# First batch's keys and queries prepared side by side in borrowed buffers, mostly transposed by DMA, with weight steps placed behind score tiles

## The chip, the cores and the metric

The kernel runs on one core of a Trainium2 chip. The metric is the time on the device in microseconds (us). The engines are TensorE (PE, with its weight loads shown apart as PEld), VectorE (DVE), ScalarE (ACT), GpSimd (POOL) and SyncE (SP). SP and ACT issue the DMAs: SP the transposes and the stores, ACT the loads.

## The reference

The inputs are `q`, `k`, `v` of 4 batches x 8 heads x 768 rows x 64, 16 `centroids` for each head, and two weights that arrive as 64-bit words.

```python
q_assign = argmax(q_n . c_n)      # q_n, k_n, c_n: normed; per head, 16 clusters
k_assign = argmax(k_n . c_n)
mask     = q_assign[..., :, None] == k_assign[..., None, :]
scores   = where(mask, q @ k.T / 8, -1e9);  attn = softmax(scores)
x = (attn @ v)  ->  3072 tokens x 512          # heads side by side
h = x @ w_in;   g = max(h, 0) + log1p(exp(-|h|));   out = g @ w_out   # 2048 wide
```

So each row of a query sees only the keys of its own cluster, and a softplus feed-forward follows.

## The kernel before, in words

All large products run in fp16 as a high and a low half. The mask is put into the product: a transposed key or query has 128 rows, of which 64 hold the values (T0: low and high half; T1: the high half beside 16 mask columns of -65504 or 0), so that scores come out masked.

Work is cut into 8 passes: batch b, and three of its six row tiles (`QT = 3`). A pass has 8 heads x 3 = 24 score tiles of 128 x 768. For a tile, `scores` does four matmuls (L544), the row maximum on DVE (`negm`, L560) and the exponential on ACT (L568). In pass 0 the probabilities stay in fp32, are transposed on PE (L585) and copied out by ACT and DVE (L591, L593); from pass 1 on they are split into halves on ACT and POOL (`phl`, L607, L609), and two tiles at a time, 24 blocks of 128 x 128, are transposed by a DMA into `pt`. `attend` multiplies by `v` (L647 in pass 0, L651 to L653 afterwards), and `xn` is transposed by DMA into `xT`. `ffn1` (L720 to L722), `softplus` (L739 to L763) and `ffn2` (L784 to L786) of a pass run while later passes attend.

Preparation. `prep_k(n)` takes two heads of a batch: load, high half on ACT (L423), low half on POOL (L425) into a tile `n1`; transpose into `kt[:, 0]`; similarities with the centroids on PE (L394, L395); nearest centroid on DVE (L399 to L403, L440), the mask columns (L444) and a copy into a second tile `n2`; transpose into `kt[:, 1]`. `clusters` counts with a matmul (L456) which clusters have a key (`al`, L461, L464). `prep_q(n, pi)` does the same for four heads and three row tiles (L481, L485, then DVE steps and POOL's product L516). Below, k0, k2, k4, k6 are the four key pairs of batch 0, and q0, q4 its two query groups for pass 0. `turn` transposes 12 blocks, either by DMA or, for `n < NPE` (8: all of batch 0), on PE with two copies out of PSUM (L376, L380, L382). There are two `n1` and two `n2` buffers, two `raw` ones, four `kt`, two `qt`; PSUM has two banks `h` (transposes, similarities, `ffn1`), and one `o` for `ffn2`.

`prep_weights(step)` turns 64-bit words into fp16 halves: ACT, three DVE operations (L305, L309, L315), ACT, POOL (L319), in 32 steps: 16 for `w_in`, 16 for `w_out`. The words are staged in rooms of `wo` that are not yet needed; the last two steps stage in a buffer `wraw` of the ring `phl`.

The order on each engine is set before the run by a planner, `Order`. Each piece of work is a generator that yields operations with an engine and a cost in ns, and waits. The planner always emits the operation that can start first by its own prices; among equals the lower priority number goes first. `wait` and `ring` belong to the planner: they fix when it may emit. The semaphores in the program come from the data alone. Engines then run in the order emitted. Before, a transpose was priced at

```python
self.dma = max(self.dma, start + 900) + opt["dma"]     # 180 ns a block
end = max(self.dma, start + ns) + 1500
```

and a weight step had priority `begin - 12 + step * 0.6`, that is 22 + 0.6 step, where tile t has priority t.

Of the kernel before, what the change touches and what calls it, by code (L numbers as in the profile page):

```python
# [19 lines left out]
DDS = 1024  # L20
LAG = 4
AHEAD = 10
NPE = 8
# [4 lines left out]
class Order:  # L28
# [8 lines left out]
    def __init__(self):  # L37
        self.free = dict.fromkeys(self.LAT, 0.0)
        self.ev, self.blocked, self.active = {}, {}, []
        self.dma = 0.0  # L40
        self.shared = {"DVE": 0.0, "POOL": 0.0}
        self.rings = {}
        self.cur, self.seq = None, 0
# [7 lines left out]
    def get(self, tag, size):  # L51

        k = self.rings.get(tag, 0)
        self.rings[tag] = k + 1
        return ("wait", (tag, k - size)) if k >= size else None, (tag, k)
# [24 lines left out]
    def run(self):  # L80
        while self.active:
# [27 lines left out]
def tile_cluster_attention__then__softplus_ffn(  # L109
# [18 lines left out]
    SH = S // 2  # L128
    QT = 3

    passes = [(b, c0) for b in range(B) for c0 in range(0, NT, QT)]
    NF = DFF // P
    SCALE = 1.0 / math.sqrt(D)
    nb = QT * P

# [67 lines left out]
    def load(dst, src, nbytes):  # L203
        return op("ACT", 60, lambda: nc.scalar.dma_start(dst, src), dma=nbytes / 290.0)

    def flip(dst, src, blocks):

        return op(
            "SP", 150 * blocks + 100, lambda: nc.sync.dma_start_transpose(out=dst, in_=src), dma=180.0 * blocks
        )  # L210
# [4 lines left out]
    def prep_centroids():  # L215
# [8 lines left out]
        yield op("DVE", 150, lambda: V.tensor_tensor(sq, cf, cf, ALU.mult), dma=0)  # L224
# [45 lines left out]
    def prep_weights(step: int):  # L270
# [60 lines left out]
    def raw_tile(nm, n, shape):  # L331

        if n < H and nm != "q":
# [3 lines left out]
        return key, p2.tile(shape, F32, tag="raw", name=f"raw{nm}_{n}")  # L337

# [26 lines left out]
    def turn(dst, src, name: str, on_chip: bool):  # L365
# [4 lines left out]
        for g in range(0, dst.shape[1], NT):  # L370
            hk = yield from ring("h", 2)
            ps = ps_h.tile([P, NT, P], F16, tag="h", name=f"{name}_{g}")

            def emit(g=g, ps=ps):
                for c in range(NT):
                    nc.tensor.transpose(out=ps[:, c], in_=src[:, g + c], identity=eye)  # L376

            yield op("PE", 350, emit)
            if g:
                yield op("DVE", 950, lambda g=g, ps=ps: nc.vector.tensor_copy(dst[:, g : g + NT], ps))  # L380
            else:
                yield op("ACT", 820, lambda g=g, ps=ps: nc.scalar.copy(dst[:, g : g + NT], ps))  # L382
            od.set(hk)

    def nearest(xs, heads, low: int, sfx: str):
# [3 lines left out]
        ps = ps_h.tile([P, 2 * nt, NCL], F32, tag="h", name=f"sim_{sfx}")  # L389
        sim = ps[:, :nt]  # L390
# [7 lines left out]
        mx = p2.tile([P, nt, 1], F32, tag="mx", name=f"mx_{sfx}")  # L398
# [3 lines left out]
        best = p2.tile([P, nt, 1], F32, tag="best", name=f"best_{sfx}")  # L402
        yield op("DVE", 345, lambda: nc.vector.tensor_reduce(best, sim, AX.X, ALU.max))  # L403
        return ps, sim, best.to_broadcast(shp)

    def next_n2():
        key = yield from ring("n2", 2)
        return key, N2[key[1] % 2]
# [3 lines left out]
    def prep_k(n: int):  # L412
# [5 lines left out]
        nk = yield from ring("n1", 2)  # L418
        kt = p2.tile([P, 2, 2, NT, P], F16, tag="kt", name=f"kt_{n}", bufs=NP)
        kT[n], kT[n + 1] = kt[:, :, 0], kt[:, :, 1]  # L420
        n1 = p2.tile([P, 2 * NT, P], F16, tag="n1", name=f"kn1_{n}")
# [10 lines left out]
        od.set(nk)  # L432
# [3 lines left out]
        ps, sim, best = yield from nearest(  # L436
            [kt0[:, c] for c in range(2 * NT)], [h] * NT + [h + 1] * NT, 2, f"k{n}"
        )
        eq = p2.tile([P, 2 * NT, NCL], F16, tag="eq", name=f"eq_k{n}")
        yield op("DVE", 345, lambda: nc.vector.tensor_tensor(eq, sim, best, ALU.is_equal))  # L440
        yield op(
            "DVE",
            250,
            lambda: nc.vector.tensor_scalar(n2[:, :, D : D + NCL], eq, 1.0, MASK, ALU.subtract, ALU.mult),  # L444
            shared=True,
        )
        od.spawn(clusters(n, ps, eq, hk), od.cur["prio"])
        yield from turn(kt[:, 1].rearrange("p h c t -> p (h c) t"), n2, f"kT1_{n}", n < NPE)
        od.set(n2k)
        od.set(("k", n))  # L450

    def clusters(n, ps, eq, hk):
# [6 lines left out]
        al = alive[n - h % 4][:, h % 4 : h % 4 + 2]  # L459
        yield op(  # L460
            "DVE", 345, lambda: nc.vector.tensor_reduce(al, cnt.rearrange("p (u c) l -> p u l c", u=2), AX.X, ALU.max)  # L461
        )
        od.set(hk)
        yield op("DVE", 150, lambda: nc.vector.tensor_scalar(al, al, 1.0, None, ALU.min), shared=True)  # L464
        od.set(("al", n))

    def prep_q(n: int, pi: int):

        sfx = f"{n}_{pi}"
        c12 = 4 * QT  # L470
        qkey[n, pi] = yield from ring("qt", 2)
        yield wait("kn", n + 2)
        rk, qf = yield from raw_tile("q", n, [P, 4, QT, D])
        yield load(qf, rows(q, n, passes[pi][1], QT, 4), P * c12 * D * 4)
        qf = qf.rearrange("p h c d -> p (h c) d")
        nk = yield from ring("n1", 2)
        qt = p2.tile([P, 2, 4, QT, P], F16, tag="qt", name=f"qt_{sfx}")
        for u in range(4):
            qT[n + u, pi] = qt[:, :, u]
        n1 = p2.tile([P, c12, P], F16, tag="n1", name=f"qn1_{sfx}")  # L480
# [9 lines left out]
        yield from turn(qt0, n1, f"qT0_{sfx}", pi == 0 and n < NPE)  # L490
        heads = [(n + c // QT) % H for c in range(c12)]
        yield wait("cents")
        yield wait("al", n)
        yield wait("al", n + 2)
        n2k, n2 = yield from next_n2()
        hk = yield from ring("h", 2)
        ps, sim, best = yield from nearest([qt0[:, c] for c in range(c12)], heads, 1, f"q{sfx}")
# [3 lines left out]
        sim4 = sim.rearrange("p (u c) l -> p u c l", u=4)  # L501
        al = alive[n]
# [4 lines left out]
                sim4, sim4, al.unsqueeze(2).to_broadcast([P, 4, QT, NCL]), ALU.mult  # L507
# [11 lines left out]
        od.set(nk)  # L519
        yield from turn(qt[:, 1].rearrange("p h c t -> p (h c) t"), n2, f"qT1_{sfx}", pi == 0 and n < NPE)  # L520
        od.set(n2k)
# [3 lines left out]
    steps = [(b * H + h, pi) for pi, (b, _) in enumerate(passes) for h in range(H)]  # L525
    tiles = [(n, pi, i) for n, pi in steps for i in range(QT)]
    pair, sums = {}, {}

    def scores(t: int):
        n, pi, i = tiles[t]  # L530
        sfx = f"{n}_{passes[pi][1] + i}"
# [23 lines left out]
        if i == QT - 1 and n % 2 and passes[pi][1] + QT == NT:  # L555
            od.set(kkey[n // 2])
        if i == QT - 1 and n % 4 == 3:
# [6 lines left out]
        if pi == 0:  # L564
            if n // 2 not in sums:
                sums[n // 2] = p2.tile([P, 2 * QT, 1], F32, tag="sum", name=f"sum_{n}", bufs=NP)
            tot["accum_out"] = sums[n // 2][:, n % 2 * QT + i]
        yield op("ACT", 900, lambda: nc.scalar.activation(p32, st[:, :, :SH], AF.Exp, bias=negm, **tot))  # L568
        od.set(sk)
        if pi == 0:  # L570
# [8 lines left out]
            for j in range(2):  # L579
# [7 lines left out]
                yield op("PE", 640, emit)  # L587
# [7 lines left out]
            if t == H * QT - 1:  # L595
# [33 lines left out]
    def attend(t: int):  # L629
        n, pi, i = tiles[t]  # L630
        h = n % H
# [6 lines left out]
        if h % 2 == 0 and i == 0:  # L638
            avs["k"] = yield from ring("m", 1)
            avs["t"] = ps_m.tile([P, 2, QT, D + 1], F32, tag="m", name=f"av_{n}_{pi}")  # L640
# [14 lines left out]
        yield op("PE", 1300 if pi == 0 else 530, emit)  # L655
# [3 lines left out]
        if h % 2 == 0 or i < QT - 1:  # L659
            return  # L660
# [221 lines left out]
```

## Time and profile before

| | |
|---|---|
| Median of 3 runs | 906.68 us (903.77 to 907.39) |
| Profiled execution | 904.0 us, its span 902.2 us |
| PE / DVE / ACT / POOL busy | 91% / 62% / 65% / 58% of the span |
| Mean granted clock of PE | 0.973 |
| DMA | 136.02 MB, mean 151 GB/s |

A row of a group of instructions gives the line, the engine, the operation, what is written from what, the count, then busy us and mean ns of one, then idle time just before and what ended it. A row by stretch gives the start and end, the length, the busy us of PE, PEld, DVE, ACT and POOL with their counts, the granted clock, the share of DMA and its GB/s. A row of one line's instructions gives min/median/max in ns and the first and last start. Rows of the chain that ended last, and of the order in time, begin with start and length. A row of waits gives who waited for whom, us in total, how often, the longest. The page's rows of DMA issues end with the median us from issue to landing. SPq and ACTq are the queues of those engines' DMA issues.

### The profile page before, as it was taken

The page shows a single profiled execution, that of the slowest core. Times are in us where ns is not written, and L with a number is a line of the kernel's source. Part 1 is how long each engine was busy: PE and PEld are TensorE (multiplying, and loading weights), DVE is VectorE, ACT ScalarE, POOL GpSimd, SP SyncE. Part 2 cuts the span into 40 slices and gives each one's busy share as a digit, 9 for nine tenths or more (in the row PEclk, how much of TensorE's full clock was granted, in tenths as well). Part 3 has the DMA queues.
Part 4 walks back from the last instruction along what each step waited for, and adds up shares of the span by engine and source line. Part 5 has one row for each costly group of instructions (what it writes and reads, how often), then busy time and mean ns, then how long its engine had stood idle before and what let it go on. Part 6 is the DMA issues. An engine that isn't in the chain of part 4 may idle for free.

```text
span 902.2 us, 19238 instructions
## 1 busy us (share of the span) xinstructions
PE 823.7 (91%) x7843; PEld 520.0 (58%) x7843; DVE 560.8 (62%) x1034; ACT 589.4 (65%) x904; POOL 523.9 (58%) x353
## 2 busy tenths in 40 slices
PE   2669797889679999999999999999999999999996
PEld 2558684555335666666666666666666666655542
DVE  5889787778685665675766666666665645433331
ACT  5657477886458877876767777867677676633320
POOL 5233326896548778777677676776676565512210
PEclk9979699999799999999999999999999999999998
DMA  6323439999546979999888779998867755600000
GB/s 222 95 94 120 130 128 195 199 226 237 141 123 159 202 171 202 223 203 230 157 199 179 162 149 206 207 211 182 171 155 161 133 115 138 126 9 25 12 1 35
DMA packets 393320, 136.02 MB, mean 151 GB/s; under 512 B 369680, under 2 KB 386064, under 8 KB 393232
## 3 DMA queue, kind: packets, MB, share of 16 engines
q1 hardware_dynamic: 371472, 99.15, 54.9%
q10 hardware_dynamic: 21760, 35.66, 13.0%
q8 instruction: 61, 1.00, 0.5%
q14 instruction: 27, 0.22, 0.1%
HBM read 35.68 MB, written 6.29 MB: 47 GB/s over the span
## 4 chain that ended last, share of the span: by engine, by line
PE 72%; DMA 4%; DVE 3%; POOL 3%; issue 2%; ACT 2%; POOLq 0%; DVEq 0%; ACTq 0%
PE s L544 10%; PE o L786 9%; PE o L784 9%; PE o L785 9%; PE h L720 8%; PE h L722 8%; PE h L721 8%; PE av L651 3%; PE av L653 3%; PE av L652 3%; DMA pt<-phl 3%; POOL phl L609 2%; DMA xT<-xn 1%; ACT p L568 1%; DVE negm L560 1%
## 5 line engine op out<-in xcount | busy, mean ns | idle before, releaser
L609 POOL TENSOR_TENSOR phl<-p,phl 128x768 f16<-128x768 f32 x168 | 277.2, 1666 | 90.9 <-ACT phl L607 54.2
L560 DVE TENSOR_REDUCE negm<-s 128x1 f32<-128x768 f32 x192 | 182.9, 954 | 67.5 <-PE s L544 65.2
L568 ACT ACTIVATE p<-s,negm 128x768 f32<-128x768 f32 x192 | 172.3, 898 | 72.9 <-DVE negm L560 47.7
L763 POOL TENSOR_TENSOR gh<-fg,gh 128x768 f16<-128x768 f32 x64 | 105.7, 1652 | 134.5 <-ACT gh L762 134.0
L720 PE MATMUL h<-xT,wi 128*128 128x384 f16 x512 | 167.9, 328 | 14.6 <-DVE fg L751 6.2
L722 PE MATMUL h<-xT,wi 128*128 128x384 f16 x512 | 168.1, 328 | 0.0
L721 PE MATMUL h<-xT,wi 128*128 128x384 f16 x512 | 168.0, 328 | 0.0
L544 PE MATMUL s<-kt,qt 128*128 128x384 f16 x768 | 158.5, 330 | 10.2 <-ACT p L568 10.0
L784 PE MATMUL o<-wo,gh 128*128 128x512 f16 x384 | 146.3, 381 | 4.9 <-ACT gh L762 3.3
L786 PE MATMUL o<-wo,gh 128*128 128x512 f16 x384 | 146.5, 382 | 1.4 <-POOL gh L763 1.4
L785 PE MATMUL o<-wo,gh 128*128 128x512 f16 x384 | 146.4, 381 | 0.1
L741 ACT ACTIVATE fa<-fa 128x384 f32<-128x384 f32 x128 | 66.6, 521 | 114.8 <-DVE fa L739 114.1
L607 ACT CAST phl<-p 128x768 f16<-128x768 f32 x168 | 134.1, 827 | 7.1 <-DMA pt<-phl 5.5
L739 DVE TENSOR_SCALAR fa<-h 128x384 int32<-128x384 int32 x128 | 71.1, 556 | 104.0 <-PE h L722 102.8
L651 PE MATMUL av<-vb,pt 128*128 128x65 f16 x1008 | 108.7, 192 | 1.9 <-DMA pt<-phl 1.8
L652 PE MATMUL av<-vb,pt 128*128 128x64 f16 x1008 | 108.7, 192 | 0.0
L653 PE MATMUL av<-vb,pt 128*128 128x65 f16 x1008 | 108.4, 194 | 0.0
L544 PEld LDWEIGHTS <-qt 128*128 128x128 f16 x768 | 72.7, 99 | 58.5 <-issue 15.1
L751 DVE SCALAR_TENSOR_TENSOR fg<-h,fa 128x384 f32<-128x384 f32 x128 | 70.6, 552 | 57.1 <-ACT fa L742 54.5
L651 PEld LDWEIGHTS <-pt 128*128 128x128 f16 x1008 | 93.6, 98 | 15.7 <-DMA pt<-phl 3.4
L652 PEld LDWEIGHTS <-pt 128*128 128x128 f16 x1008 | 92.9, 97 | 11.8
L653 PEld LDWEIGHTS <-pt 128*128 128x128 f16 x1008 | 93.1, 97 | 0.0
(114 smaller groups left out, 1193.6 us busy)
## 6 DMA issues: line engine op xcount, KB each, us to landing
wo<-in_moe_w_in_dram ACTq DMA_DIRECT2D x16, 512.0 KB, 3.6
wo<-in_moe_w_out_dram ACTq DMA_DIRECT2D x14, 512.0 KB, 3.9
rawk<-in_k_dram ACTq DMA_DIRECT2D x16, 384.0 KB, 4.8
rawv<-in_v_dram ACTq DMA_DIRECT2D x16, 384.0 KB, 4.8
rawq<-in_q_dram ACTq DMA_DIRECT2D x16, 384.0 KB, 4.2
out_dram<-ot SPq DMA_DIRECT2D x24, 256.0 KB, 2.5
pt<-phl SPq DMA_TRANSPOSE x84, 5.5
wraw<-in_moe_w_out_dram ACTq DMA_DIRECT2D x2, 512.0 KB, 3.7
```

The lines of the kernel that those rows point to most:

```text
L544: nc.tensor.matmul(st[:, j, :SH], qt[:, s, i], kt[:, s, NT // 2 * j : NT // 2 * (j + 1)], start=(s == 0), stop=(s == 1),)
L560: yield op("DVE", 950, lambda: nc.vector.tensor_reduce(negm, st[:, :, :SH], AX.XY, ALU.max, negate=True))
L609: "POOL", 1640, lambda: nc.gpsimd.tensor_tensor(phl[:, u, 1], p32, phl[:, u, 0], ALU.subtract), shared=True
L651: nc.tensor.matmul(av, pt[:, 0, c], vb[:, c, D : 2 * D + 1], start=(c == 0), stop=False)
L652: nc.tensor.matmul(av[:, :D], pt[:, 0, c], vb[:, c, :D], start=False, stop=False)
L653: nc.tensor.matmul(av, pt[:, 1, c], vb[:, c, D : 2 * D + 1], start=False, stop=(c == NT - 1))
L720: nc.tensor.matmul(hp, w[0], x[0], start=(c == 0), stop=False)
L721: nc.tensor.matmul(hp, w[0], x[1], start=False, stop=False)
L722: nc.tensor.matmul(hp, w[1], x[0], start=False, stop=(c == NP - 1))
L784: nc.tensor.matmul(po, g[0], wo[:, f, 0, 0], start=(f == f0), stop=False)
L785: nc.tensor.matmul(po, g[0], wo[:, f, 0, 1], start=False, stop=False)
L786: nc.tensor.matmul(po, g[1], wo[:, f, 0, 0], start=False, stop=(f == f0 + NF // 2 - 1))
```

## The change

1. `NPE` becomes `(2, 4, 0, 0)`: on PE remain the T0 transposes of k0 and of q0. The ten others of batch 0 go by DMA through SP.
2. `part_tiles` gives `n1` and `n2` of batch 0 in pass 0 other homes: k0 and q0 use the two rings, k2 and q4 take the two `phl` buffers, k4 and k6 the two `xT` buffers. POOL clears the unused columns of those four.
3. q's similarities in pass 0 use the PSUM bank `o`, and wait for `al` only before the multiplication with it.
4. A key's comparison is made in place in PSUM, and the mask is made from PSUM and no longer from a fp16 tile `eq`; the count then multiplies the mask columns, and `al` is the maximum compared with -65504 x 128.
5. A weight step waits in the planner until tile `-8 + 1.4 step` is scored (the first six do not), and has priority `1.4 step - 4`.
6. The planner's prices change: transposes and loads are two streams, a block costs 148 ns, twice that while the other stream is at work, and the landing 1200; `attend` in pass 0 costs 680 and no longer 1300, a PE transpose of probabilities 330 and no longer 640, the exponential in pass 0 1095. `ffn2` waits for `g` before it takes the bank `o`.
7. `QT` becomes a number kept by each pass (`FIRST = 3` for batch 0, so the same).

```diff
+WGATE = -8
+WPACE = 1.4
+WDUE = 4
-NPE = 8
+FIRST = 3
+NPE = (2, 4, 0, 0)
...
-            if "dma" in opt:
-                self.dma = max(self.dma, start + 900) + opt["dma"]
-                end = max(self.dma, start + ns) + 1500
+            if "flip" in opt:
+                self.flips = max(self.flips, start + 900) + opt["flip"] * (2.0 if self.loads > start else 1.0)
+                end = max(self.flips, start + ns) + 1200
+            if "load" in opt:
+                self.loads = max(self.loads, start + 1200) + opt["load"] * (2.0 if self.flips > start else 1.0)
+                end = self.loads + 1200
...
-            "SP", 150 * blocks + 100, lambda: nc.sync.dma_start_transpose(out=dst, in_=src), dma=180.0 * blocks
+            "SP", 150 * blocks + 100, lambda: nc.sync.dma_start_transpose(out=dst, in_=src), flip=148.0 * blocks
...
+        gate = int(WGATE + step * WPACE)
+        if gate >= 0:
+            yield wait("sc", gate)
         yield op("ACT", 630, lambda: nc.scalar.activation(mag, val, AF.Abs, scale=sc))
...
+    homes = {("k", 0): None, ("q", 0): None, ("k", 2): "phl", ("q", 4): "phl", ("k", 4): "xT", ("k", 6): "xT"}
+    def part_tiles(nm, n, pi, blocks):
+        tag = homes.get((nm, n)) if pi == 0 else None
+        sfx = f"{nm}{n}_{pi}"
+        if tag is None:
+            k1 = yield from ring("n1", 2)
+            k2 = yield from ring("n2", 2)
+            n1 = p2.tile([P, blocks, P], F16, tag="n1", name=f"n1_{sfx}")
+            return [k1, k2], n1, N2[k2[2] % 2][:, :blocks]
+        key = yield from ring(tag, 2)
+        both = p2.tile([P, 2, blocks, P], F16, tag=tag, name=f"n12_{sfx}")
+        nc.gpsimd.memset(both[:, 1, :, D + NCL :], 0.0)
+        return [key], both[:, 0], both[:, 1]
...
-        yield from turn(kt0, n1, f"kT0_{n}", n < NPE)
+        yield from turn(kt0, n1, f"kT0_{n}", n < NPE[0])
...
-        yield op("DVE", 345, lambda: nc.vector.tensor_tensor(eq, sim, best, ALU.is_equal))
-            lambda: nc.vector.tensor_scalar(n2[:, :, D : D + NCL], eq, 1.0, MASK, ALU.subtract, ALU.mult),
+        yield op("DVE", 345, lambda: nc.vector.tensor_tensor(sim, sim, best, ALU.is_equal))
+        mask = n2[:, :, D : D + NCL]
+        yield op("DVE", 345, lambda: nc.vector.tensor_scalar(mask, sim, 1.0, MASK, ALU.subtract, ALU.mult))
+        od.spawn(clusters(n, ps, mask, hk), od.cur["prio"])
+        yield from turn(kt[:, 1].rearrange("p h c t -> p (h c) t"), n2, f"kT1_{n}", n < NPE[2])
...
-        yield op("PE", 100, lambda: nc.tensor.matmul(cnt, ones, eq, start=True, stop=True))
+        yield op("PE", 100, lambda: nc.tensor.matmul(cnt, ones, mask, start=True, stop=True))
+        yield op("DVE", 190, lambda: nc.vector.tensor_scalar(al, top, -MASK * P, None, ALU.is_gt))
...
-        yield wait("al", n)
-        yield wait("al", n + 2)
-        n2k, n2 = yield from next_n2()
-        hk = yield from ring("h", 2)
+        if pi:
+            yield wait("al", n)
+            yield wait("al", n + 2)
+            hk = yield from ring("h", 2)
+            ps = ps_h.tile([P, c12, NCL], F32, tag="h", name=f"sim_q{sfx}")
+        else:
+            hk = yield from ring("o", 1)
+            ps = ps_o.tile([P, c12, NCL], F32, tag="o", name=f"sim_q{sfx}")
...
-        yield op("PE", 1300 if pi == 0 else 530, emit)
+        yield op("PE", 680 if pi == 0 else 530, emit)
...
+        yield wait("g", pi, NF // 4 * half)
         ok = yield from ring("o", 1)
...
-        od.spawn(prep_weights(step), begin - 12 + step * 0.6)
+        od.spawn(prep_weights(step), WGATE + WDUE + step * WPACE)
```

More of the change, by code (lines that the diff above doesn't have):

```diff
@@ L54, in get @@
         self.rings[tag] = k + 1
-        return ("wait", (tag, k - size)) if k >= size else None, (tag, k)
+        return ("wait", ("ring", tag, k - size)) if k >= size else None, ("ring", tag, k)
     def spawn(self, gen, prio):
@@ L129, in tile_cluster_attention__then__softplus_ffn @@
     QT = 3
-    passes = [(b, c0) for b in range(B) for c0 in range(0, NT, QT)]
+    passes = [(b, c0, nt) for b in range(B) for nt in (FIRST if b == 0 else QT,) for c0 in range(0, NT, nt)]
     NF = DFF // P
     SCALE = 1.0 / math.sqrt(D)
-    nb = QT * P
     ctx.enter_context(tc.manual_schedule())
@@ L369, in turn @@
             return
-        for g in range(0, dst.shape[1], NT):
+        step = dst.shape[1] // 2
+        for g in range(0, dst.shape[1], step):
             hk = yield from ring("h", 2)
-            ps = ps_h.tile([P, NT, P], F16, tag="h", name=f"{name}_{g}")
+            ps = ps_h.tile([P, step, P], F16, tag="h", name=f"{name}_{g}")
             def emit(g=g, ps=ps):
-                for c in range(NT):
+                for c in range(step):
                     nc.tensor.transpose(out=ps[:, c], in_=src[:, g + c], identity=eye)
@@ L518, in prep_q @@
         )
-        od.set(nk)
-        yield from turn(qt[:, 1].rearrange("p h c t -> p (h c) t"), n2, f"qT1_{sfx}", pi == 0 and n < NPE)
-        od.set(n2k)
+        yield from turn(qt[:, 1].rearrange("p h c t -> p (h c) t"), n2, f"qT1_{sfx}", pi == 0 and n < NPE[3])
+        for key in keys:
+            od.set(key)
         od.set(("q", n, pi))
-    steps = [(b * H + h, pi) for pi, (b, _) in enumerate(passes) for h in range(H)]
-    tiles = [(n, pi, i) for n, pi in steps for i in range(QT)]
+    steps = [(b * H + h, pi) for pi, (b, _, _) in enumerate(passes) for h in range(H)]
+    tiles = [(n, pi, i) for n, pi in steps for i in range(passes[pi][2])]
+    last = [c0 + nt == NT for _, c0, nt in passes]
     pair, sums = {}, {}
@@ L553, in scores @@
         od.set(("sc", t))
-        if i == QT - 1 and n % 2 and passes[pi][1] + QT == NT:
+        if i == nt - 1 and n % 2 and last[pi]:
             od.set(kkey[n // 2])
-        if i == QT - 1 and n % 4 == 3:
+        if i == nt - 1 and n % 4 == 3:
             od.set(qkey[n - 3, pi])
@@ L565, in scores @@
             if n // 2 not in sums:
-                sums[n // 2] = p2.tile([P, 2 * QT, 1], F32, tag="sum", name=f"sum_{n}", bufs=NP)
-            tot["accum_out"] = sums[n // 2][:, n % 2 * QT + i]
-        yield op("ACT", 900, lambda: nc.scalar.activation(p32, st[:, :, :SH], AF.Exp, bias=negm, **tot))
+                sums[n // 2] = p2.tile([P, 2 * nt, 1], F32, tag="sum", name=f"sum_{n}", bufs=NP)
+            tot["accum_out"] = sums[n // 2][:, n % 2 * nt + i]
+        yield op("ACT", 1095 if pi == 0 else 900, lambda: nc.scalar.activation(p32, st[:, :, :SH], AF.Exp, bias=negm, **tot))
         od.set(sk)
@@ L630, in attend @@
         n, pi, i = tiles[t]
+        nt = passes[pi][2]
         h = n % H
@@ L707, in ffn1 @@
         w0 = f * P % WC
+        nb = passes[pi][2] * P
         for pr in range(NP):
@@ L817, in tile_cluster_attention__then__softplus_ffn @@
     od.spawn(prep_centroids(), -30)
-    first = {}
+    first, begin = {}, []
     for t, (n, pi, i) in enumerate(tiles):
         first.setdefault((n, pi), t)
-    for pi, (b, c0) in enumerate(passes):
+    for pi, (b, c0, nt) in enumerate(passes):
+        begin.append(first[b * H, pi] + H * nt + AHEAD)
         for h in range(0, H, 2):
```

137 lines of the change are left out of this document (63 added, 74 removed).

## The prediction

> **What bounds the kernel now.** I read the page's head first, then the stretches of time between the first maxima of the passes, then the stretches one by one.
>
> ```profile
> span 902.2 us, 19238 instructions
> ...
> PE   2669797889679999999999999999999999999996
> ...
> PEclk9979699999799999999999999999999999999998
> DMA  6323439999546979999888779998867755600000
> ...
> q1 hardware_dynamic: 371472, 99.15, 54.9%
> q10 hardware_dynamic: 21760, 35.66, 13.0%
> ...
> qt<-qn SPq DMA_TRANSPOSE x14, 4.6
> qt<-n SPq DMA_TRANSPOSE x14, 3.4
> kt<-kn SPq DMA_TRANSPOSE x12, 5.0
> kt<-n SPq DMA_TRANSPOSE x12, 3.6
> ```
>
> From the twelfth slice on PE stands at 9; before it there are holes in PE's busy digits and dips of its clock. So the kernel is bound by TensorE after some 250 us and by something else before. The boundaries come from the row maxima of the scores (24 tiles a pass), the sums from the busy times by stretch:
>
> ```profile
> L560 DVE TENSOR_REDUCE negm<-s x24: 914/948/958, 55.5 to 130.6; 128x1 f32<-128x768 f32 x24
> ...
> L560 DVE TENSOR_REDUCE negm<-s x24: 945/954/959, 132.2 to 200.6; 128x1 f32<-128x768 f32 x24
> ...
> 0.00:55.50 55.50, 24.52 (x300) 20.25 (x301) 39.19 (x115) 28.60 (x41) 22.64 (x23) 0.91 0.45 148
> 55.50:131.60 76.10, 67.56 (x509) 57.55 (x507) 67.34 (x110) 50.39 (x102) 21.95 (x20) 0.89 0.39 116
> 131.60:200.60 69.00, 56.44 (x615) 37.48 (x613) 51.24 (x85) 57.84 (x87) 54.88 (x37) 1.00 0.97 201
> 200.60:253.60 53.00, 41.79 (x410) 24.49 (x409) 38.19 (x73) 28.02 (x47) 30.85 (x21) 0.87 0.87 202
> 253.60:880.00 626.40, 618.74 (x5963) 374.63 (x5961) 362.43 (x650) 423.75 (x628) 391.96 (x253) 1.00 0.71 150
> ```
>
> The columns are length, then busy PE, PEld, DVE, ACT, POOL, the granted clock, the DMA share. Five stages: preparation (55.5 us, PE busy 24.5); pass 0 (76.1 us, DVE busy 67.3); pass 1 (69.0 us, DMA share 0.97); a gap of 53.0 us with no score tile, in which PE does the first feed-forward and runs short; and 626.4 us in which PE idles 7.7. What a faster start can bring is PE idle time of the first four stages: 31.0 + 8.5 + 12.6 + 11.2 = 63.3 us, and some slow clock. All later work only moves.
>
> **The preparation: 14 us taken off.** The first score tile waits for query tile q0, and q0 comes late:
>
> ```profile
> 13.26 1.64 POOL L425 TENSOR_TENSOR kn<-rawk,kn 128x768 f16<-128x768 f32 x1 [2.59 <-ACT kn L423]
> ...
> 30.11 0.84 ACT L481 ACTIVATE qn<-rawq 128x768 f16<-128x768 f32 x1
> ...
> 44.05 0.36 DVE L399 TENSOR_REDUCE mx_q<-sim_q 128x12 f32<-128x192 f32 x1 [0.16 <-PE sim_q L395]
> ...
> 48.33 3.34 POOL L516 TENSOR_TENSOR n<-qn,aq 128x768 f16<-128x768 f16 x2 [4.09 <-DVE aq L511]
> ...
> 54.03 2.27 PE L544 MATMUL s<-kt,qt 128*128 128x384 f16 x8
> ```
>
> L481, q0's first step, starts at 30.11: the two n1 buffers were going round among four key pairs before. With buffers of their own (n1, n2, phl, xT) nothing of the four pairs and two query groups waits for another's buffer. The new chain, from these rows: k2's second half is there at 13.26 + 1.64 = 14.9; its transpose by DMA takes 5.0 (kt<-kn), to 19.9; eight DVE steps of 0.36 and some 1.2 us of similarities and count on PE, together 4.1, to 24.0; q0, whose own similarities run beside this in the o bank, then needs two DVE steps (0.7), POOL's product (1.7, half of 3.34) and a transpose (qt<-n 3.4): 29.8. Two other transposes ahead of it on SP's queue, at 1.5 of issue each, make it about 33. That is the end with undisturbed transposes.
>
> The other end is a loaded DMA. Ten transposes of 12 blocks move from PE to SP's queue:
>
> ```profile
> 80.40 1.32 SPq L209 DMA_TRANSPOSE xT<-xn  x1
> ...
> L209 SPq DMA_TRANSPOSE qt<-qn x14: 1430/1474/2460, 90.9 to 694.6; - x14
> ```
>
> The first row is SP's first transpose of the run, the second gives the ns of issue. So SP is empty here, but each transpose waits in order for its producer. Their cost in DMA time: q1 moved 99.15 MB in 54.9% of 902.2 us, 5.0 us a MB, so 1.96 us for 0.393 MB; q10 moved 35.66 MB in 13.0%, 3.3 us a MB, 1.29 us for a key or query load and 1.72 for a weight load. Twelve loads, seven transposes that tile 0 or its neighbours in the queue need, and seven weight loads make 15.5 + 13.7 + 12.0 = 41.2 us, if all stand ahead of tile 0. How a transpose fares at a full DMA shows in the chain that ended last, in pass 1:
>
> ```profile
> 144.97 8.12 DMA xT<-xn
> ...
> 194.87 8.75 DMA pt<-phl
> ```
>
> With 8.75 us instead of 5.0 and 3.4 the chain is 9.1 longer, 42. I take 40, near the loaded end, since the DMA share of the first slice is already 0.6 and the transposes come on top: 54.0 - 40 = 14.0 us. The ends are 21 and, should the queue order hold q0's last transpose behind all ten (ten times 1.96 after 14.9, plus a loaded 8.75, plus the 7 us of steps), 50: 4 us.
>
> The Trainium skill (DMA: Bandwidth & Descriptors, section Issuing engines are not separate DMA queues) states that DMAs of different issuers run on the same 16 engines and interleave, which speaks against this part. By it the first tile would come at 41, by the undisturbed medians at 33; the 8.12 and 8.75 us above agree with it.
>
> PE loses 120 of 144 transposes, ACT and DVE ten copies each:
>
> ```profile
> L382 ACT COPY kt<-kT 128x768 f16<-128x768 f16 x8 | 6.4, 798 | 3.6 <-PE kT L376 3.5
> ...
> L380 DVE COPY kt<-kT 128x768 f16<-128x768 f16 x8 | 4.4, 555 | 3.2 <-PE kT L376 3.0
> ...
> L444 DVE TENSOR_SCALAR n<-eq_k x16: 198/209/1648, 19.2 to 628.2; 128x192 f16<-128x192 f16 x16
> ```
>
> That is 10 x 0.56 = 5.6 us of DVE and 8.0 of ACT, both in a stage where they have 16 and 27 us idle: nothing of its own beyond the chain above. The mask from PSUM costs one of the 0.36 steps instead of 0.21, but the old form reached 1.65; 16 times in the run, and under PE afterwards: nothing. Four more memsets on POOL come before its first real work: nothing.
>
> **Pass 0: 6.4 us lost.** This stage is DVE's, and the earlier start does not remove DVE work, it moves it:
>
> ```profile
> L560 DVE TENSOR_REDUCE negm<-s 128x1 f32<-128x768 f32 x24 | 22.7, 948 | 3.7 <-PE s L544 3.6
> L315 DVE SCALAR_TENSOR_TENSOR wo<-wo 128x512 int32<-128x512 int32 x16 | 14.1, 882 | 0.1
> L591 DVE COPY ptf<-pT 128x384 f32<-128x384 f32 x23 | 12.7, 551 | 3.3 <-PE pT L585 3.2
> L309 DVE SCALAR_TENSOR_TENSOR wo<-wo,wi 128x512 int32<-128x512 int32 x11 | 8.1, 734 | 0.2
> ...
> L319 POOL TENSOR_TENSOR wi<-wo,wi x16: 1150/1159/1320, 28.3 to 111.6; 128x512 f16<-128x512 f32 x16
> ...
> L319 POOL TENSOR_TENSOR wo<-wo x14: 1148/1157/1260, 114.1 to 259.5; 128x512 f16<-128x512 f32 x14
> L319 POOL TENSOR_TENSOR wo<-wraw,wo x2: 1151/1152/1152, 265.3 to 272.2; 128x512 f16<-128x512 f32 x2
> ```
>
> (The first four rows are DVE in 55.5 to 131.6.) Some 15 weight steps run here at about 1.9 us of DVE. The wait on "sc" is a wait of the planner alone: no semaphore comes from it, it sets a step's place in the queues. Step s may start once tile -8 + 1.4 s is scored and ranks as tile 1.4 s - 4, so by tile 24 step 20 is due; the old order had 20 by then too. Six are ungated and fall into the preparation, so 14 remain in pass 0, 1.4 less (2.6 us). But k4, k6 and q4 must now be finished beside the tiles: 2 x 7 DVE steps of 0.36 and two short ones of 0.2, and for q4 8 x 0.36 and a pass over 768 columns, by the maxima 0.95: together 9.3. DVE: 67.3 - 2.6 + 9.3 = 74.0, and 8.5 idle against 8.8: 82.5 instead of 76.1. Bounds: 76 if the leftovers fit into the preparation, 88 if 22 steps come. Tile 24 then at 124.
>
> **Pass 1 and the gap: 12 us taken off, and 4 behind it.** The DMA share, 0.97 x 69.0 + 0.87 x 53.0 = 113 of 122.0 us, sets how far this can shrink. Some four weight loads move ahead (4 x 1.72): floor 106, so at most 16. What ends the gap is seen in the waits of 200 to 254 us:
>
> ```profile
> ACT wo L318 <- DVE wo L315: 11.2, 3, 4.7
> ...
> PE h L720 <- DVE aq L511: 5.4, 1, 5.4
> ...
> SPq L209 <- POOL wo L319: 15.2, 2, 9.6
> ```
>
> Late weight steps sit in front of the second batch's masks on DVE and of the transposes that SP must issue in order. The new order has all steps due by tile 40, so the last comes in pass 1 instead of at 272 us; ffn2 of pass 0 gets its second half of weights in time. What is late next is k10's chain, which starts only when pass 1 has scored tile 35 and frees a kt buffer. Three quarters of the 16: 12; at least 0, when that chain rules. Of the 7.7 us of PE idle after 253.6 I take 4, since the last two steps (wraw) no longer hold a phl buffer there. They hold it in pass 1 instead, for one or two pairs; that is paid out of the quarter.
>
> **Everything else** (the planner's other prices, the renamed sizes, ffn2's wait for g ahead of the o bank): the instructions stay, their order changes. Where PE is full the order costs nothing as long as pt arrives in time; if that cover goes, it is the third rival.
>
> **Sum:** -14.0 + 6.4 - 12.0 - 4.0 = -23.6 against this execution's own 904.0 us: 880. It lies 2.7 us below the median of the runs, 906.68, which I leave as scatter (903.8 to 907.4).
>
> **The rivals.**
> First, tighter packing: tile 0 at 33 (-21), leftovers hidden (0), the gap at its DMA floor (-16), all PE idle behind it gone (-7): 904 - 44 = 860. For it: PE and DMA have room before 130 us (shares 0.45 and 0.39). Against: every stage at its floor.
> Second, no change. The gap keeps its end: tile 48 hangs on a chain of four transposes behind pass 1, the DMA there is full, and an earlier start turns into a longer gap. With tile 0 at 50 (-4) and pass 0 at +6: 906.
> Third, slower, by one mechanism: the planner now prices a transpose at 0.148 us a block plus 1.2, for the 24 blocks of a pt tile 4.75 us when it sees no load (5.8 before), while the profile has a median of 5.5:
>
> ```profile
> pt<-phl SPq DMA_TRANSPOSE x84, 5.5
> ```
>
> PE runs in order; if attend is placed that much too early, each of the 72 pt tiles of the full stage stalls PE. At 0.75 us each that is 54 us, and 904 - 24 + 54 = 934. It decides from (24 + 4.5) / 72 = 0.4 us a tile on. Against: attend runs four tiles behind scores, and PE idled only 7.7 us there at prices of both kinds.
>
> **How the numbers follow.** The sum as worked out 0.50 (866 to 896), tighter packing 0.25, no change 0.11, slower 0.14. About 4.5 us either way (0.5% of 906.68, where the runs spread over 3.6) is what can be told from no change: faster 0.76, same 0.11, slower 0.13. The range leaves out the slower rival and the lower part of the first one: 856 to 906.
>
> **What would show it.** First scores at about 40 us, with L481 for q0 before 20; if later than 50, the transposes are in each other's way. Tile 24's maximum at 124; below 115 my DVE sum is wrong. The last weight step (the POOL subtraction) before 200. Tile 48 at about 234. PE idle under 8 us from there on; tens of us, ended by pt transposes, would be the third rival. Wrong altogether it is if pass 0 stretches as much as the start shrinks and the gap stays at 53.

## The result, and the profile after

The kernel after takes 934.76 us (931.20 to 939.15), the kernel before, run beside it, 906.31: a ratio of 1.032, 95% interval 1.0271 to 1.037. The change costs 28 us; 880 was forecast. Times here and below are medians of several executions; one of run 12's four, at 930.42 us, was in a slower state and is left out of its time and ratio. The profiled execution after is 931.2 us long, 27.2 more than that of before by the spans.

The page of the kernel after, to be read against the first fence of the prediction:

```profile
span 929.4 us, 19015 instructions
...
PE   2298877889669998999999999999999999999996
...
DMA  7936379999769899999987889998986766620000
...
q1 hardware_dynamic: 387152, 103.08, 62.1%
...
L678 PE MATMUL av<-vb,pt 128*128 128x65 f16 x1008 | 111.5, 194 | 16.9 <-DMA pt<-phl 16.8
...
pt<-phl SPq DMA_TRANSPOSE x84, 6.6
```

The same row of `attend` on the page of the kernel before:

```profile
L651 PE MATMUL av<-vb,pt 128*128 128x65 f16 x1008 | 108.7, 192 | 1.9 <-DMA pt<-phl 1.8
```

The first two slices of DMA stand at 7 and 9 tenths now, where they stood at 6 and 3, as meant. But PE waits 16.8 us for `pt` where it waited 1.8, a transpose of 24 blocks lands after 6.6 us instead of 5.5, and the queue q1 takes 62.1% of the 16 engines' span instead of 54.9%, for 3.93 MB more. By the stretches between the first maxima of the passes, first after, then before (length, then busy PE, PEld, DVE, ACT, POOL, the granted clock, the DMA share):

```profile
0.00:43.90 43.90, 10.52 (x180) 8.22 (x181) 30.80 (x100) 18.82 (x28) 24.38 (x26) 1.00 0.89 224
43.90:118.20 74.30, 65.93 (x478) 55.42 (x477) 57.02 (x99) 46.25 (x96) 18.20 (x16) 0.89 0.45 114
118.20:262.70 144.50, 112.83 (x1055) 70.25 (x1055) 102.76 (x173) 96.53 (x149) 97.30 (x66) 0.88 0.92 193
262.70:807.30 544.60, 524.66 (x5386) 321.76 (x5383) 329.09 (x592) 381.70 (x561) 366.74 (x237) 0.99 0.89 166
```

```profile
55.50:132.20 76.70, 68.16 (x511) 57.70 (x508) 67.89 (x110) 50.98 (x103) 22.55 (x20) 0.89 0.40 117
132.20:253.70 121.50, 97.73 (x1020) 61.84 (x1020) 88.89 (x156) 85.38 (x133) 85.13 (x57) 0.94 0.93 201
253.70:780.60 526.90, 521.15 (x5382) 322.77 (x5381) 328.99 (x591) 387.75 (x568) 371.39 (x240) 1.00 0.83 174
```

Tile 0 comes 11.6 us earlier, pass 0 is 2.4 shorter, the stretch from tile 24 to tile 48 is 23.0 longer, the one from tile 48 to the last tile 17.7 longer, and the tail 0.5: together +27.2, the difference of the spans. Two losses have to be explained.

### The profile page after: what moved, and what is told of

It is laid out like the page before. It is cut to its first block, busy times and chain, and to the rows that moved or that the text cites. A ratio compares the mean times of both kernels' runs of the same rounds, so it can differ in the third digit from the quotient of the medians.

```text
span 929.4 us, 19015 instructions
## 1 busy us (share of the span) xinstructions
PE 826.3 (89%) x7723; PEld 513.1 (55%) x7723; DVE 555.5 (60%) x1024; ACT 580.0 (62%) x894; POOL 528.8 (57%) x357
## 3 DMA queue, kind: packets, MB, share of 16 engines
q1 hardware_dynamic: 387152, 103.08, 62.1%
## 4 chain that ended last, share of the span: by engine, by line
PE 62%; DMA 16%; DVE 10%; issue 4%; ACT 4%; POOL 2%; SPq 1%; POOLq 0%; ACTq 0%; DVEq 0%
DMA pt<-phl 14%; PE s L570 9%; PE o L814 7%; PE o L816 7%; PE o L815 7%; PE h L748 7%; PE h L749 7%; PE h L750 7%; PE av L674 3%; PE av L678 2%; PE av L680 2%; PE av L679 2%; DVE negm L586 2%; ACT p L594 2%; PE pT L611 1%
## 5 line engine op out<-in xcount | busy, mean ns | idle before, releaser
L748 PE MATMUL h<-xT,wi 128*128 128x384 f16 x512 | 170.3, 333 | 15.4 <-DVE fg L780 12.1
L570 PE MATMUL s<-kt,qt 128*128 128x384 f16 x768 | 162.7, 337 | 15.9 <-ACT p L594 12.4
L749 PE MATMUL h<-xT,wi 128*128 128x384 f16 x512 | 170.5, 333 | 0.0
L750 PE MATMUL h<-xT,wi 128*128 128x384 f16 x512 | 170.3, 333 | 0.0
L678 PE MATMUL av<-vb,pt 128*128 128x65 f16 x1008 | 111.5, 194 | 16.9 <-DMA pt<-phl 16.8
L678 PEld LDWEIGHTS <-pt 128*128 128x128 f16 x1008 | 94.8, 99 | 36.4 <-DMA pt<-phl 25.0
L679 PE MATMUL av<-vb,pt 128*128 128x64 f16 x1008 | 111.4, 194 | 0.0
L680 PE MATMUL av<-vb,pt 128*128 128x65 f16 x1008 | 111.0, 196 | 0.0
L679 PEld LDWEIGHTS <-pt 128*128 128x128 f16 x1008 | 94.4, 98 | 10.9 <-issue 0.3
L680 PEld LDWEIGHTS <-pt 128*128 128x128 f16 x1008 | 94.6, 98 | 0.0
```

The lines of the kernel that those rows point to most:

```text
L570: nc.tensor.matmul(st[:, j, :SH], qt[:, s, i], kt[:, s, NT // 2 * j : NT // 2 * (j + 1)], start=(s == 0), stop=(s == 1),)
L678: nc.tensor.matmul(av, pt[:, 0, c], vb[:, c, D : 2 * D + 1], start=(c == 0), stop=False)
L679: nc.tensor.matmul(av[:, :D], pt[:, 0, c], vb[:, c, :D], start=False, stop=False)
L680: nc.tensor.matmul(av, pt[:, 1, c], vb[:, c, D : 2 * D + 1], start=False, stop=(c == NT - 1))
L748: nc.tensor.matmul(hp, w[0], x[0], start=(c == 0), stop=False)
L749: nc.tensor.matmul(hp, w[0], x[1], start=False, stop=False)
```

## The experiments

**The layout.** The wait for `pt` begins with the transposes themselves. SP's issue of `pt<-phl` (ns, min/median/max), before and after:

```profile
L209 SPq DMA_TRANSPOSE pt<-phl x84: 2892/3098/7172, 141.8 to 785.1; - x84
```

```profile
L215 SPq DMA_TRANSPOSE pt<-phl x84: 3481/3782/8076, 131.0 to 811.8; - x84
```

Even the shortest one went from 2.89 to 3.48 us, with the same shape and the same source ring. What differs is the address. Rings get their place in SBUF in the order in which their first tile is allocated, and `part_tiles` now allocates `phl` early. In the built kernels the two `phl` buffers stand at bytes 210688 and 216832 of a partition before (multiples of 256), at 168832 and 174976 after (128 off). The transpose reads rows of 128 fp16, that is 256 bytes (on the page before, q1 moves 99.15 MB in 371472 packets, 267 bytes each on average). Theory: a row that straddles two blocks of 256 bytes costs more. Rival: the loaded DMA slows the transposes, wherever they read.

Run 1 puts `phl` of the kernel before 128 bytes off; the planner doesn't see addresses, and by the traces the order of the instructions on every engine is that of the kernel before.

```diff
+            if not padded:
+                padded.append(p2.tile([P, 64], F16, tag="pad", name="pad", bufs=1))
             pair[t // 2] = p2.tile([P, 2, 2, 2, SH], F16, tag="phl", name=f"phl_{sfx}"), key
```

> The kernel before, with one unused buffer of 128 bytes a partition laid ahead of the phl buffers, so that the 256-byte rows that the pt transposes read begin 128 bytes off a multiple of 256 (as they do in the changed kernel); no instruction is added and the order is the same. Theory A (layout: rows read off a multiple of 256 make the transposes slower): issue of a pt transpose after 300 us from a median of 3.1 to 3.7 us, its landing from 5.5 to 6.5, PE begins to wait for pt in the full stage, time 906 + 10 to 18: 916 to 924. Theory B (the planner's lower price of a transpose, so the order of instructions): no change, issue 3.1, 904 to 908.

Measured: 912.04 against 906.81, ratio 1.0052 (1.0022 to 1.0082).

```profile
L209 SPq DMA_TRANSPOSE pt<-phl x84: 3403/3710/8992, 140.9 to 791.9; - x84
```

From its page:

```profile
q1 hardware_dynamic: 371472, 99.15, 60.5%
...
L655 PE MATMUL av<-vb,pt 128*128 128x65 f16 x1008 | 109.7, 193 | 8.8 <-DMA pt<-phl 7.8
...
pt<-phl SPq DMA_TRANSPOSE x84, 6.5
```

Issue and landing are what theory A forecast, with the same order of instructions, so a fuller DMA is not needed to slow them. The time lies between the two ranges; PE waits 7.8 us for `pt`, half of what it waits in the kernel after.

Run 2 does the reverse: after, with pads ahead of `phl` (and of `xT`), so that `phl` starts at multiples of 256. The order is that of the kernel after.

```diff
         key = yield from ring(tag, 2)
+        if (nm, n) in (("k", 2), ("k", 4)):
+            p2.tile([P, 64], F16, tag=f"pad{tag}", name=f"pad_{tag}", bufs=1)
```

> The changed kernel, with an unused buffer of 128 bytes ahead of phl and another behind it, so that phl alone begins at a multiple of 256. Theory A: issue of a pt transpose back to 3.1 us, landing 5.5, PE waits for pt in the full stage nearly gone, time 910 to 918 (the 9 us lost before tile 48 stay in part). Theory B: 931 to 939, issue 3.7.

Measured: 919.35, ratio 1.0139 (1.01 to 1.0179), instead of 1.032. The landing is back to 5.8 us, the wait of PE for `pt` to 4.6.

```profile
L215 SPq DMA_TRANSPOSE pt<-phl x84: 2943/3162/8727, 132.1 to 799.5; - x84
```

The time is 1.35 us above the upper end of theory A's range.

Run 3 puts every buffer that a transpose reads, and `kt`, `qt` and `xT` that it writes, at multiples of 256, by a pad among the constants and one ahead of `xn`.

> The changed kernel, with the pads placed so that every buffer that a transpose reads (n1, n2, phl, xn) and kt, qt, xT begin at a multiple of 256. Theory A: e2 and some us less, since the T0 transposes of k and q read n1 rows that are 128 bytes off in both kernels: 903 to 914. Theory B: 931 to 939.

Measured: 914.92, ratio 1.0098 (1.0068 to 1.0129), again about 1 us above theory A's range. From its page:

```profile
q1 hardware_dynamic: 387152, 103.08, 56.5%
...
L679 PE MATMUL av<-vb,pt 128*128 128x65 f16 x1008 | 110.3, 193 | 2.8 <-DMA pt<-phl 2.8
...
pt<-phl SPq DMA_TRANSPOSE x84, 5.6
```

The wait for `pt` is 2.8 us again, the landing 5.6, and a MB on q1 costs 56.5% of 912.0 / 103.08 = 5.0 us as before the change (62.1% of 929.4 / 103.08 = 5.6 after). The stretch from tile 48 on is nearly what it was too:

```profile
118.30:259.50 141.20, 111.77 (x1054) 69.30 (x1054) 103.19 (x173) 96.01 (x150) 97.01 (x66) 0.89 0.92 198
259.50:789.20 529.70, 521.29 (x5387) 321.95 (x5383) 329.28 (x591) 381.19 (x561) 367.12 (x237) 0.99 0.82 171
```

So the layout is worth 20 us of the 28 in the order of the change, and 5 in the order of before: the same slower transposes, but there they are mostly hidden. It is most of the second loss, 14.9 of its 17.7 us (529.7 against 544.6; 526.9 before the change), and little of the first, 3.3 of 23.0 (141.2 against 144.5; 121.5 before). The runs compare multiples of 256 with 128 bytes off and no other offset, so that it is the straddling of a block is still a theory.

Run 4 asks whether the kernel before has something to gain as well: its `n1` and `kt` stand 128 off, and a pad among the constants puts them at multiples of 256 (`al` gets three buffers instead of four to make the room).

> The kernel before, with a pad ahead of its buffers, and one al buffer less, so that n1 and kt begin at a multiple of 256 and all from qt on stays where it was. Theory A: landing of kt<-kn and qt<-qn from 5.0 and 4.6 to about 4.0, time 900 to 906, a gain of a few us in the gap before tile 48. Theory B: 904 to 908.

Measured: 905.76, ratio 0.9986 (0.9962 to 1.001). Nothing that can be told: what those two rings cost by their place is small or hidden there. The landing of `kt<-kn`, which theory A put at 4.0, went from 5.0 to 4.7.

**The parts, on the aligned kernel.** Run 3's kernel is the base of all that follows; 9 us over the kernel before remain. Run 5 takes the wait behind tiles out of the weight steps and gives them the old priority:

```diff
-        gate = int(WGATE + step * WPACE)
-        if gate >= 0:
-            yield wait("sc", gate)
...
-        od.spawn(prep_weights(step), WGATE + WDUE + step * WPACE)
+        od.spawn(prep_weights(step), H * QT + AHEAD - 12 + step * 0.6)
```

> e3 (the changed kernel with all transposed buffers at multiples of 256), and the weight steps placed as before: no wait on sc, priority 22 + 0.6 step. What is left of the loss after e3 is 8 us; it sits between tile 24 (118 us) and tile 48 (260 us). Theory W (the new placing puts 11 weight steps between tiles 24 and 47, where the old had 6, and makes that pass 89 us long instead of 69): 898 to 908, the pass below 80 us. Theory P (the planner's new prices of transposes and loads): 912 to 918. Theory N (the first batch's ten transposes by DMA): 912 to 918. Theory C (the order is a matter of chance within some us, whatever is changed): anything from 905 to 925, without the pass following the steps.

Measured: 932.24, ratio 1.026 (1.0204 to 1.0317), above the range of every theory. Run 6 goes back to one DMA stream in the planner, 180 ns a block and a landing of 1500:

```diff
-            if "flip" in opt:
...
+            if "flip" in opt or "load" in opt:
+                self.flips = max(self.flips, start + 900) + opt.get("flip", opt.get("load"))
+                end = max(self.flips, start + ns) + 1500
...
-            "SP", 150 * blocks + 100, lambda: nc.sync.dma_start_transpose(out=dst, in_=src), flip=148.0 * blocks
+            "SP", 150 * blocks + 100, lambda: nc.sync.dma_start_transpose(out=dst, in_=src), flip=180.0 * blocks
```

> e3, and the planner's prices of transposes and loads as before (one stream, 180 ns a block, landing 1500). W: 912 to 918. P: 898 to 908, fewer and shorter waits of PE for pt and of SP for its producers. N: 912 to 918. C: 905 to 925.

Measured: 916.46, ratio 1.0101 (1.0045 to 1.0158). Run 7 transposes the first batch on PE again (`NPE = (8, 8, 8, 8)`).

> e3, and all transposes of the first batch on PE again (NPE 8 in all four places), still in buffers of their own. My prediction: the first tile comes some us later or earlier than the 43.7 of e3, by the chain without any transpose of 5 us, at about 38 to 46. W and P: 910 to 918. N: 900 to 908. C: 905 to 925.

Measured: 931.13, ratio 1.0254 (1.0183 to 1.0324), above every range as well. Run 8 goes back to the old prices of the work in pass 0:

```diff
-        yield op("ACT", 1095 if pi == 0 else 900, lambda: nc.scalar.activation(p32, st[:, :, :SH], AF.Exp, bias=negm, **tot))
+        yield op("ACT", 900, lambda: nc.scalar.activation(p32, st[:, :, :SH], AF.Exp, bias=negm, **tot))
...
-                yield op("PE", 330, emit)
+                yield op("PE", 640, emit)
...
-        yield op("PE", 680 if pi == 0 else 530, emit)
+        yield op("PE", 1300 if pi == 0 else 530, emit)
```

> e3, and the planner's prices of attend and of the PE transposes in pass 0, and of the exponential, as before (1300, 640, 900). By W the placing of the weight steps follows the tiles, so this moves little: 910 to 918. P and N: 912 to 918. A fourth theory, that the old price left air in pass 0 that the weight steps used: 900 to 908 with more steps before tile 24 than the 15 of e3. C: 905 to 925.

Measured: 905.54, ratio 0.9969 (0.9937 to 1.0002), as the fourth theory has it (900 to 908), and with 17 weight steps started before tile 24 instead of 15.

**How much is chance.** Each of these edits gives another order on all engines. Runs 9 and 10 change the price of a transposed block from 148 ns to 150 and 146 on the aligned kernel, runs 11 and 12 from 180 to 182 and 178 on the kernel before: edits without a meaning.

> e3 with the planner's price of a transposed block at 150 ns and not 148, a nudge that has no meaning of its own. Theory D (the 8 us that e3 loses, and what e5 to e8 moved, belong to the parts changed): 912 to 918, as e3. Theory C (any change of a price reshuffles the order before tile 48, and the time moves by as much as e5 to e8 did): off e3 by 8 us or more in one of e9 and e10, with tile 48 off the 259.5 us of e3.

> e3 with the price of a transposed block at 146 ns. D: 912 to 918. C: as for e9, and not the same time as e9.

> The kernel before with the price of a transposed block at 182 ns and not 180. D: 904 to 908. C: off 906 by 8 us or more in one of e11 and e12; slower rather than faster, if the order of the kernel before is a lucky one among its neighbours.

> The kernel before with the price of a transposed block at 178 ns. D: 904 to 908. C: as for e11.

Measured: 925.14, ratio 1.0197 (1.0155 to 1.024), and 924.19, 1.0201 (1.0162 to 1.024), where the base is at 1.0098; 910.84, 1.0055 (1.003 to 1.008), and 920.21, 1.0148 (1.0083 to 1.0213), on the kernel before. A nudge of 1% moves the time by 5 to 14 us. No single run of the parts above can be read against that, so two of the three large effects were repeated under the same nudges, 13 and 14 for the old prices of pass 0, 15 and 16 for the old order of the weights (150 in 13 and 15, shown here, 146 in 14 and 16):

```diff
-            "SP", 150 * blocks + 100, lambda: nc.sync.dma_start_transpose(out=dst, in_=src), flip=148.0 * blocks
+            "SP", 150 * blocks + 100, lambda: nc.sync.dma_start_transpose(out=dst, in_=src), flip=150.0 * blocks
```

> The aligned kernel with the old prices of attend, of the transposes on PE and of the exponent, and the price of a DMA transpose at 150 ns a block instead of 148. Theory A, the old prices are worth 9 us by themselves: the kernel stays 9 to 15 us under the aligned kernel at 150 (925.1), so 905 to 916 on this run's kernel before of about 906.5. Theory B, the 905.5 of the old prices at 148 was a chance of the written-out order: anywhere from 905 to 930, and not nearer to 905 than the aligned kernel's own three (914.9, 925.1, 924.2).

> As the run at 150, with 146 ns a block. Theory A: 905 to 916. Theory B: anywhere from 905 to 930; one of the two above 918 would be enough for it, both under 912 would be enough for theory A.

> The aligned kernel with the weight steps in the old order and without their wait behind tiles, and 150 ns a block. Theory A, the weight steps held behind tiles gain some 17 us here and the old order costs that: 932 or more, that is 7 or more above the aligned kernel at 150 (925.1) and at 146 (924.2). Theory B, chance: 905 to 932, as likely below 925 as above.

> As the run at 150, with 146 ns a block. Theory A: 932 or more. Theory B: 905 to 932; either of the two under 922 would speak for theory B.

Measured, ratios to the kernel before in the same runs:

| price of a block | 148 | 150 | 146 |
|---|---|---|---|
| aligned | 1.0098 (1.0068 to 1.0129) | 1.0197 (1.0155 to 1.024) | 1.0201 (1.0162 to 1.024) |
| old prices of pass 0 | 0.9969 (0.9937 to 1.0002) | 1.0014 (0.9984 to 1.0044) | 1.0029 (1.0006 to 1.0052) |
| old weight order | 1.026 (1.0204 to 1.0317) | 1.0122 (1.0081 to 1.0163) | 1.025 (1.02 to 1.0299) |

The old prices gain 1.3, 1.8 and 1.7%, some 15 us: an effect of their own. The old weight order gives +1.6, -0.8 and +0.5%: no sign that holds, so the loss of run 5 can't be put down to it. Runs 6 and 7 were not repeated and stay undecided: what the transposes by DMA are worth by themselves is not known.

**Why the prices matter.** What PE takes in pass 0, by groups of the kernel before (busy us, mean ns):

```profile
L647 PE MATMUL av<-rawv,ptf 128*128 128x64 f32 x288 | 37.8, 284 | 0.1
L585 PE MATMUL pT<-eye,p 128*128 128x128 f32 x144 | 25.4, 303 | 6.0 <-ACT p L568 2.3 <-DVE aq L511 2.1 <-DVE ptf L591 1.1
```

A tile has one `attend` (37.8 / 24 = 1.58 us) and two transposes of three blocks (25.4 / 48 = 0.53 each), 2.6 us. The old prices are 1.3 + 2 x 0.64 = 2.6; the new ones 0.68 + 2 x 0.33 = 1.3. Over 24 tiles the planner counts 31 us of PE work too little. Run 17 puts only the new prices into the kernel before; run 18 puts 1575 and 510, close to the rows, into the aligned kernel and keeps the new price of the exponential.

> The kernel before with the three new prices of pass 0 (attend 680, a transpose of probabilities on PE 330, the exponential 1095) and nothing else changed. Theory A, the new prices are too low for what PE does there (1.6 us and 0.51 us by the rows) and order the first two passes badly by themselves: 9 us or more above the kernel before, so 916 or more, and tile 48 later than its 253.7. Theory B, they only do harm together with the rest of the change (first batch's transposes by DMA, weight steps behind tiles): 902 to 915, the spread of the kernel before under a nudge of a price.

> The aligned kernel with the prices that the rows give for pass 0: attend 1575, a transpose of probabilities 510, the exponential at 1095 as in the change. Theory A, a price near what PE takes there is what the old prices had right: 903 to 912, with tile 48 at 225 to 240 as in the three runs with old prices. Theory B, it was something about the old numbers themselves: 912 to 925, with tile 48 at 246 or later.

Measured: 926.2, ratio 1.0199 (1.0145 to 1.0253), and 905.62, ratio 0.9976 (0.9949 to 1.0003). Both runs came out as the theory has it, from both sides and in two surroundings. Run 17 by itself proves little, as run 12 got nearly as far by chance, and its tile 48 came at 258.1, only 4 us later; but all eight aligned kernels with the low prices stand at 1.0098 or above, and all four with higher ones at 1.0029 or below. As run 18 keeps the exponential's new price, it is the two prices of PE work that matter.

What the low price does can be seen in the weight steps. POOL's last step of `w_in`, the sixteenth of 32, in the kernel after, the aligned one, run 18 and run 17, in this order:

```profile
L328 POOL TENSOR_TENSOR wi<-wo,wi x16: 1148/1162/1862, 26.3 to 124.8; 128x512 f16<-128x512 f32 x16
```

```profile
L329 POOL TENSOR_TENSOR wi<-wo,wi x16: 1149/1158/1861, 26.1 to 124.9; 128x512 f16<-128x512 f32 x16
```

```profile
L329 POOL TENSOR_TENSOR wi<-wo,wi x16: 1147/1158/1857, 27.8 to 116.0; 128x512 f16<-128x512 f32 x16
```

```profile
L319 POOL TENSOR_TENSOR wi<-wo,wi x16: 1152/1164/1456, 28.1 to 164.9; 128x512 f16<-128x512 f32 x16
```

With the low price this step starts at 124.8, after tile 24 (118.2); in run 18 at 116.0, before its tile 24 (123.9); in run 17 at 164.9, where the kernel before had 111.6. By tile 24, 17 steps have started in each of the four kernels with the higher prices, and 15, 15, 13 and 12 in runs 3, 9, 10 and 17. The planner's own times, which the kernel's text fixes, agree: in run 3 it has tile 24 scored at 103.8 us and the sixteenth step done at 112.0, in run 18 at 120.2 and 113.0; on the chip tile 24 comes at 118.3 and 123.9. The planner thinks that the tiles run faster than PE can, and puts their steps ahead of weight steps that the real engines would have had time for. These fall into pass 1, where the DMA share is 0.92. In run 18 the stretch from tile 24 to 48 is 38 us shorter than in run 3:

```profile
123.90:227.20 103.30, 83.93 (x849) 52.72 (x848) 81.54 (x133) 76.20 (x116) 80.71 (x53) 0.93 0.93 204
227.20:784.00 556.80, 541.12 (x5546) 332.93 (x5545) 345.93 (x622) 395.66 (x586) 381.40 (x247) 0.99 0.84 172
```

Of that, 27 us come back behind tile 48, where 19.8 us more of PE work are done (541.12 against 521.29) with 7.3 us more idle: the boundary between the two moves with the order, and only the end counts, 784.0 against 789.2 here.

How two weight steps more by tile 24 become some 15 us at the end is not shown. A gain is there by tile 72, which comes at 315 to 321 us in the four kernels with the higher prices and at 331 to 338 in runs 3, 9 and 10. The last steps are no earlier for it, by these rows of the kernel after and of run 18:

```profile
L328 POOL TENSOR_TENSOR wo<-wraw,wo x2: 1142/1146/1151, 260.6 to 273.5; 128x512 f16<-128x512 f32 x2
```

```profile
L329 POOL TENSOR_TENSOR wo<-wraw,wo x2: 1145/1148/1152, 261.9 to 275.0; 128x512 f16<-128x512 f32 x2
```

## Why the prediction was wrong, point by point

**The preparation** was right in its time: first scores forecast at 40, seen at 42.40, first maximum at 43.90, a gain of 11.6 for 14. q0's first ACT step came at 12, where "before 20" was asked. The Trainium skill (DMA: Bandwidth & Descriptors, section Issuing engines are not separate DMA queues) says that the DMAs of all issuers run on the same 16 engines, by which the prediction had 41: the trace agrees, with 42.40. In order of time, the start and length:

```profile
12.05 0.84 ACT L497 ACTIVATE n_q<-rawq 128x768 f16<-128x768 f32 x1
```

```profile
42.40 2.13 PE L570 MATMUL s<-kt,qt 128*128 128x384 f16 x6
```

But the rows by stretch show what kind of gain it is. PE was busy for 24.5 us there and is for 10.5: its idle time went from 31.0 to 33.4. The stretch got shorter by the PE work taken out of it and not by PE idling less. The prediction had counted its 14 us as idle time won.

**Pass 0** was mis-sized: forecast 82.5 us with 74.0 of DVE, measured 74.3 with 57.0. The weight steps, forecast to take 2.6 us less of DVE, took 12.4 less (33.0 before, 20.6 after, by the rows of these stretches). The largest row after, beside L315 with x16 and 14.1 us in the prediction:

```profile
L324 DVE SCALAR_TENSOR_TENSOR wo<-wo 128x512 int32<-128x512 int32 x11 | 7.5, 686 | 0.0
```

Fifteen steps and not 20 had started by tile 24. The prices account for two of the five, as run 18 has 17. And the 9.3 us of leftovers were not there: k4 and k6 were finished in the preparation, and q4's steps, 3.8 us, were in the 67.3 already and were counted twice. So the +6.4 was -2.4. That was no gain; it was work put off. The sign "below 115 my DVE sum is wrong" did not show it, as tile 24 came at 118.2.

**Pass 1 and the gap, -12 forecast, +23.0 measured**, is the first step that failed; tile 48 came at 262.7 and not at 234. Of the 23.0, 7.9 are PE idling more and 15.1 more PE work: 35 matmuls more, where pass 0 has 33 fewer, at a granted clock of 0.88 instead of 0.94. The forecast rested on "by tile 24 step 20 is due; the old order had 20 by then too" and on weights that end before 200; the last step came at 273.5. A due tile is a wait and a priority in the planner and no date: its own times have 14 steps done by tile 24 and the last at 251.7. Better prices alone do not mend that, as run 18 has its last step at 275.0.

The term put at nothing stands under "Everything else": "Where PE is full the order costs nothing as long as pt arrives in time". It covers the new prices of pass 0, 680 for 1300 and 330 for 640, though PE idles 8.5 and 23.8 us in the two stretches before tile 48, and the prediction did not set them beside the rows that give 1575 and 530. They measured some 15 us (mean ratio 1.0165 of the aligned kernels at three block prices, 0.9997 of the four with higher prices of pass 0: 1.7% of 907); run 3 against run 8 alone gives 12 by their ratios.

**PE idle behind it, -4 forecast**, is the second step that failed: the stretch is 17.7 us longer, of which 14.2 are PE idling (19.9 where it was 5.8). The same sentence was the ground, and `pt` did not arrive in time. PE waiting for `pt` is what the third rival forecast, but not by its cause, the planner's price of a transpose: run 3 keeps that price and the whole order, moves only the buffers, and the wait falls from 16.8 to 2.8 us. The transposes really became slower, by an address that the diff does not show.

**The third rival's 934** agrees with the 934.76 by coincidence: 54 us of waits were worked out, 16.8 are there, and the rest has another cause.

**One reading** in the prediction is off by a slice: PE's digits stand at 9 from the thirteenth slice on and not from the twelfth. Nothing hangs on it.

**Together:** from 1.032 to 1.0098 by the layout (20 us), and on to 0.9969 (run 8) or 0.9976 (run 18) by the prices: that covers the 28 us, though part of the second step may be the scatter of the order. What is left of the change is not told apart from the kernel before, and no version beat it. Why its tile 0, 10 us earlier, brings nothing at the end is only partly shown. In run 18, PE's busy time over the span is 819.8 us where it was 823.7, although 120 transposes of 15.2 us left it, and PE idles some 8 us more. The page of run 18 names the work that takes longer:

```profile
L571 PE MATMUL s<-kt,qt 128*128 128x384 f16 x768 | 162.7, 337 | 18.6 <-ACT p L595 18.5
...
L679 PE MATMUL av<-vb,pt 128*128 128x65 f16 x1008 | 111.0, 194 | 7.6 <-DMA pt<-phl 7.6
```

and the page before:

```profile
L544 PE MATMUL s<-kt,qt 128*128 128x384 f16 x768 | 158.5, 330 | 10.2 <-ACT p L568 10.0
```

Scores take 4.2 us more and the three rows of `attend` 6.7 more, and PE waits longer for `p` and for `pt` (7.6 us instead of 1.8). Why the same matmuls take longer stays open.

## What to carry to other kernels

When a change adds or moves an allocation, compare the addresses of everything that a DMA transposes, modulo 256, before reading the times. Where a program orders the work ahead by prices, a price is part of the kernel: set it from measured rows, in the stage where it applies. And nudge a meaningless number by 1% before a few us are put down to an edit: here one run of each part would have given the new weight order a credit of 15 us that the nudged runs do not bear out.

## What the runs showed of the hardware

A transpose by DMA of 24 blocks takes SP 3.1 to 3.2 us to issue when its 256-byte rows start at multiples of 256, and 3.7 to 3.8 when they start 128 bytes off (medians of runs 1 to 3 and the two kernels); it lands after 5.5 to 5.8 or 6.5 to 6.6 us, at 5.0 to 5.1 or 5.6 us a MB of DMA time. The Trainium skill (DMA: Bandwidth & Descriptors, section How a descriptor splits into AXI transactions) says that a transaction must start at a 256-byte boundary, so that a descriptor which starts elsewhere fetches bytes that it doesn't use. By that rule a row of 256 bytes that starts 128 off is two transactions and 12 beats instead of one and 8, which is an estimate and no row of its table. The runs agree in direction; the cost measured is 12% of DMA time and 20% of issue and not a half more. The Trainium skill (DMA: Bandwidth & Descriptors, section DMA Transpose (X-bar), Constraints) asks for an alignment of 32 bytes alone, which both layouts meet.

The time of a statically planned order is sensitive to small changes of the plan: 1% on one price gave 906, 911 and 920 us for the kernel before, and 915, 925 and 924 for the aligned one.
